# Half of w_out loaded as float32 by SyncE, and q and k of the first tile loaded four tokens a partition

## The chip, the cores and the metric

The kernel runs on one core of one Trainium2 chip. The metric is the device time of one execution in microseconds; the time before is the median of three executions. A span is the time from the first to the last instruction of the one execution that was profiled.

## The reference

Chunked attention (64 tokens attend to the same 64 tokens, in each of 8 heads) is followed by a multiplicative feed-forward stage without a non-linearity, all in float32.

```python
q, k, v: (8, 8, 576, 64)            # batch, heads, tokens, head dim
scores = (1 / sqrt(64)) * q_c @ k_c.T          # per chunk of 64 tokens
attn = exp(scores - max); attn /= (sum(attn) + 1e-9)
x = (attn @ v_c) as (4608, 512)                # tokens, heads * head dim
a = x @ w1 ; b = x @ w2                        # (512, 1024) each
h = (a * b) @ w3                               # (1024, 1024)
out = h @ w_out                                # (1024, 512), float32
```

## The kernel before

The kernel works in bfloat16 with float32 accumulation. The 4608 tokens are 36 groups of 128 tokens, and four groups make one tile of 512 tokens, so there are nine tiles (`TILES`).

Since nothing stands between w3 and w_out, their product is made once on the chip, and the two last matrix products become one. `add_w3o` does this for each of the eight blocks of 128 rows of w3: TensorE transposes the block (L428), a copy brings it to SBUF (`w3t`, L226 or L228, the lines of the copy helper on ScalarE and VectorE), TensorE multiplies it with all of w_out (L439, eight matmuls of 512 columns, cut into two halves by `wo_cut`, each of which waits for its own part of w_out), and a copy stores it as `w3o_sb`.

A group (`add_group`) passes through these steps. q and k for 128 tokens are in `raw`, tokens on the partitions, heads and head dim along the row. For groups 0 to 11 TensorE transposes them (L317, eight transposes of 128x128 into one PSUM buffer `ffn`); later groups are transposed by a DMA that SP issues. k is copied to `kT`. q is copied to `qd`, a block-diagonal arrangement that has been zeroed before, in two copies of 64 partitions. Eight matmuls of 64 columns make the scores (L345), and VectorE and ScalarE do the softmax (L353 to L371). Then the probabilities are transposed (L376, or by a DMA), multiplied with v (L387), and copied to `xt`.

A tile (`add_tile`) multiplies `xt` with w1 and w2 (L471, 64 matmuls of 512 columns), multiplies the two results on VectorE (L480), and multiplies that with `w3o_sb` (L502). Outputs are copied to SBUF, the first twelve over weights that are no longer needed (`kept`), the others to 20 buffers `o_sb`. They are stored by SP after all loads are in (`OUT_AFTER`, `OUT_KEY`).

All loads are issued by POOL (GpSimd), whose DMAs convert float32 to bfloat16 on the way. Their order at the front is the list `LOADS`, written out by hand: the first half of w_out, then q and k of groups 1 and 0, the identity matrix that POOL itself makes, then blocks of w3, the second half of w_out, and so on. `load_qk` loads 128 tokens of q or k: 128 partitions by 8 heads, runs of 64 values.

The order on each engine is not found at run time. `Plan.run` walks through time with a cost for each operation (`cost`, `lag`, `issue`), a queue of eight transfers each for POOL and SP that share the transfer rate, and a key for each operation; at each moment a free engine takes the ready operation with the lowest key. The instructions are then emitted in that order, and each engine carries out its own in order. POOL takes the loads strictly in the order of the list. While the first tokens are not through, the gaps that the plan sees on TensorE are filled with matmuls on zeros (`fills`, L563), fourteen of them at the very start.

Of the kernel before, what the change touches and what calls it, by code (L numbers as in the profile page):

```python
# [16 lines left out]

LOADS = [('wo', 0, 4), ('qk', 1), ('qk', 0), ('ident',), ('w3', 7, 8), ('wo', 4, 8), ('w3', 6, 7), ('qk', 2),
# [3 lines left out]
TILES = [4] * 9  # L22
XT = 16
OUT_AFTER, OUT_KEY = 35, 80
QK_BY_DMA, A_BY_DMA = set(range(12, 36)), set(range(16, 36))
# [19 lines left out]
class Plan:  # L45
# [22 lines left out]
    def run(self):  # L68
        free = {e: 0.0 for e in ("PE", "ACT", "DVE", "POOL", "SP")}
        free["POOL"] = free["SP"] = 1.2  # L70
        todo = {e: [] for e in free}
# [9 lines left out]

        rings, flown = {"POOL": [], "SP": []}, 3.4
        left, now, order, ends = len(self.ops), 0.0, [], [1.2]
        loads = [o for o in self.ops if "POOL" in o.engines]
# [23 lines left out]
        while left or any(rings.values()):  # L108
# [13 lines left out]
            for eng in free:  # L122
                if free[eng] > now or len(rings.get(eng, ())) >= self.RING:
                    continue
                pick = [o for o in (loads[:1] if eng == "POOL" else todo[eng]) if ready(o)]
                if not pick:
                    continue
                o = min(pick, key=lambda o: (o.key, o.place))
                for e in o.engines:
                    todo[e].remove(o)  # L130
                if eng == "POOL":
                    loads.pop(0)
                o.start, o.engine = now, eng
                cost = o.cost[o.engines.index(eng)] if isinstance(o.cost, tuple) else o.cost
                if o.issue:
                    free[eng] = now + o.issue
                    rings[eng].append([free[eng], cost, o])
# [7 lines left out]
                heapq.heappush(ends, free[eng])  # L145
                left -= 1
            while ends and ends[0] <= now:
# [9 lines left out]
def kernel(  # L157
# [20 lines left out]
    B, H, S, D = q.shape  # L178
    C = 64
    NCH = S // C  # L180
    N_TOK = B * S
# [34 lines left out]

    qds = [wpool.tile([P, 2, NM, 2 * C], bf, tag=f"qd{i}", name=f"qd{i}") for i in range(BUFS["qd"])]
    vds = [wpool.tile([P, NM, NCH, 2 * D], bf, tag=f"vd{i}", name=f"vd{i}") for i in range(BUFS["vd"])]
    es = [wpool.tile([P, 8, C + 1], bf, tag=f"e{i}", name=f"e{i}") for i in range(BUFS["e"])]
    halves = [slice(0, C), slice(C, P)]  # L220
# [34 lines left out]
    def load_qk(g):  # L255
# [3 lines left out]
        for w, src in enumerate((q, k)):  # L259
            for r, b, c, n in parts:  # L260
# [4 lines left out]
                box["ops"].append(load(0.45 * n, 0.5 + 0.2 * n, emit, takes=() if box["ops"] else ("raw",)))  # L265

    def load_v(b, y0, y1):
        for t in range(2):
            def emit(eng, t=t):
                nc.gpsimd.dma_start(vds[b % len(vds)][halves[t], 2 * y0:2 * y1, :, t * D:(t + 1) * D].rearrange("p m c d -> p (m c) d"),  # L270
                                    v[b, NM * t + 2 * y0:NM * t + 2 * y1].rearrange("h (c p) d -> p (h c) d", p=C))
            o = load(1.025 * (y1 - y0), 0.5 + 0.335 * (y1 - y0), emit, takes=() if b in v_first else ("vd",),
                     after=(zero_v[b % len(vds)],))
            v_first.setdefault(b, o)
            for y in range(y0, y1):
                v_got.setdefault((b, y), []).append(o)

    def load_w12(j0, j1):
        for dst, w in ((w1_sb, moe_w1), (w2_sb, moe_w2)):
            for t in range(2):  # L280
                def emit(eng, dst=dst, w=w, t=t):
                    nc.gpsimd.dma_start(
                        dst[halves[t], :, j0 * P:j1 * P],
                        w[t * NM * D:(t + 1) * NM * D, j0 * P:j1 * P].rearrange("(m d) n -> d m n", d=D))
                o = load(0.41 * (j1 - j0), 0.62, emit)
        for j in range(j0, j1):
            w12_got[j] = o

    def load_w3(k0, k1):
        def emit(eng):  # L290
            nc.gpsimd.dma_start(w3_sb[:, k0:k1, :], moe_w3.rearrange("(ko p) n -> p ko n", p=P)[:, k0:k1, :])
        o = load(1.45 * (k1 - k0), 0.75, emit)
        for i in range(k0, k1):
            w3_got[i] = o

    def load_wo(k0, k1):
        def emit(eng):
            nc.gpsimd.dma_start(wo_sb[:, k0:k1, :], moe_w_out.rearrange("(ko p) n -> p ko n", p=P)[:, k0:k1, :])
        wo_got.append(load(0.72 * (k1 - k0), 0.75, emit))
        wo_cut.append((k0, k1))  # L300


    x_done = {}

    def add_group(g, kt, ks, ka, kv):
        box = {}
        bc = chunks(g)
        qd = qds[g % len(qds)]

        turned = g in QK_BY_DMA  # L310

        def t_emit(eng):
# [26 lines left out]
        def s_emit(eng):  # L339
            sc = box["sc"] = ps("p_sc", [P, 2, 2, 2, C])  # L340
            for cc in range(2):
# [5 lines left out]

        def flat(x):
            return x.rearrange("p cc y t k -> p (cc y t) k")

        def max_emit(eng):
            nm = box["nm"] = sb("nm", [P, 8, 1], f32, bufs=3)
            nc.vector.tensor_reduce(nm[:, :, 0], flat(box["sc"]), axis=AX.X, op=ALU.max)  # L353

        def sub_emit(eng):
            sd = box["sd"] = sb("sd", [P, 8, C], f32)
            nc.vector.tensor_sub(sd[:], flat(box["sc"]), box["nm"].to_broadcast([P, 8, C]))  # L357

# [33 lines left out]

        got = raws[g]["ops"]
        if turned:
            tr = kc = plan.add("SP", 1.75, kt, qk_turn, after=got, takes=("kqT",), uses=[(got[0], "raw")], lag=3.5, issue=1.3)
            held, cost = [(tr, "kqT")], (0.35, 0.6)
        else:
            tr = plan.add("PE", 0.46, kt, t_emit, after=got + [made_ident], takes=("ffn",), uses=[(got[0], "raw")], lag=0.2)
            held, cost = [(tr, "ffn")], (0.43, 0.66)
            kc = plan.add(("DVE", "ACT"), cost, kt, k_copy, after=(tr,), takes=("kT",), uses=held)  # L400
        q0 = plan.add(("DVE", "ACT"), cost, kt, q_copy(0), after=[tr] + zero_q, takes=("qd",), uses=held)
        q1 = plan.add(("DVE", "ACT"), cost, kt, q_copy(1), after=(tr, q0), uses=held)
        s = plan.add("PE", 0.24, ks, s_emit, after=(kc, q0, q1), takes=("p_sc",), uses=[(kc, "kqT" if turned else "kT"), (q0, "qd")],
                     lag=0.2)
        mx = plan.add("DVE", 0.69, ks, max_emit, after=(s,), lag=0.05)
# [9 lines left out]
        av = plan.add("PE", 0.24, kv, av_emit, after=[ac] + [o for b, _ in bc for y_ in (0, 1) for o in v_got[b, y_]], takes=("p_av",),  # L415
                      uses=[(ac, "at")] + [(v_first[b], "vd") for b in sorted({b for b, _ in bc})], lag=0.2)
        x_done[g] = plan.add(("ACT", "DVE"), 0.68, kv, x_copy, after=(av,), takes=("xt",), uses=[(av, "p_av")])

# [3 lines left out]
    def add_w3o(ko, key):  # L422
# [26 lines left out]
        for i, (k0, k1) in enumerate(wo_cut):  # L449
            mms.append(plan.add("PE", 0.216 * (k1 - k0), key - 0.1 * i, mm_emit(i), after=[tcp, wo_got[i]] + mms,  # L450
                                takes=() if i else ("ffn",), uses=[(tcp, "w3t")], lag=0.2))
# [4 lines left out]
    kept = [w3_sb[:, i:i + 1, :].rearrange("p a n -> p (a n)").bitcast(f32) for i in range(FO)]  # L456
    kept += [wo_sb[:, i:i + 2, :].rearrange("p a n -> p (a n)").bitcast(f32) for i in range(0, FO, 2)]

    def add_tile(g0, n, kab, ko_):
# [33 lines left out]
        for tk, x0, x1 in cols:  # L493
# [30 lines left out]

    made_ident, landing = None, 1.6
    for what, *args in LOADS:
        if what == "ident":
            made_ident = plan.add("POOL", 0.6, 0, lambda eng: make_identity(nc, ident[:]), lag=0.3)
        else:
            {"qk": load_qk, "v": load_v, "w12": load_w12, "w3": load_w3, "wo": load_wo}[what](*args)  # L530
    landing = 2.5
    for g in range(NG):
        if g not in raws:
            load_qk(g)
# [61 lines left out]
```

## Time and profile before

| what | value |
|---|---|
| median of 3 executions | 254.22 us (253.74 to 254.31) |
| the profiled execution | 252.69 us |
| its span | 250.9 us |
| PE (TensorE matmul) busy | 242.0 us, 96% |
| DVE (VectorE) busy | 178.1 us, 71% |
| ACT (ScalarE) busy | 140.2 us, 56% |
| POOL (GpSimd) busy | 102.1 us, 41% |
| read from and written to HBM | 38.80 MB and 9.44 MB |

Busy PE counts the matmuls on zeros too, and a matmul that is waiting in the pipeline, so 96% is not 96% useful work. PEld is the loading of the stationary operand, which overlaps the matmuls. The groups of instructions that the change touches, from the page: line, engine and operation, output and input, shapes and count, then busy us and mean ns of one, then idle time of the engine just before them.

```profile
L264 POOL DMA_DIRECT2D raw<-in_q_dram x40 | 34.3, 858 | 31.4 <-DMA kqT<-raw 11.8
L264 POOL DMA_DIRECT2D raw<-in_k_dram x40 | 34.3, 859 | 20.8 <-DMA vd<-in_v_dram 10.8
L439 PE MATMUL ffn<-wo_sb,w3t 128*128 128x512 bf16 x64 | 15.6, 379 | 0.4 <-DVE w3t L228 0.3
L228 DVE COPY qd<-ffn 64x512 bf16<-64x512 bf16 x14 | 5.9, 419 | 10.4 <-ACT kT L226 10.2
...
wo_sb<-in_moe_w_out_dram POOLq DMA_DIRECT2D x2, 512.0 KB, 7.1
```

The last line is of the DMA issues: the count, the KB of each as written, and the median us from issue to landing. A span is followed by what lies around it, 252.69 - 250.9 = 1.8 us in this execution.

### The profile page before, as it was taken

The page shows a single profiled execution, that of the slowest core. Times are in us where ns is not written, and L with a number is a line of the kernel's source. Part 1 is how long each engine was busy: PE and PEld are TensorE (multiplying, and loading weights), DVE is VectorE, ACT ScalarE, POOL GpSimd, SP SyncE. Part 2 cuts the span into 40 slices and gives each one's busy share as a digit, 9 for nine tenths or more (in the row PEclk, how much of TensorE's full clock was granted, in tenths as well). Part 3 has the DMA queues.
Part 4 walks back from the last instruction along what each step waited for, and adds up shares of the span by engine and source line. Part 5 has one row for each costly group of instructions (what it writes and reads, how often), then busy time and mean ns, then how long its engine had stood idle before and what let it go on. Part 6 is the DMA issues. An engine that isn't in the chain of part 4 may idle for free.

```text
span 250.9 us, 4705 instructions
## 1 busy us (share of the span) xinstructions
PE 242.0 (96%) x1771; PEld 124.8 (50%) x1771; DVE 178.1 (71%) x324; ACT 140.2 (56%) x237; POOL 102.1 (41%) x128
## 2 busy tenths in 40 slices
PE   8699989999999999999999999999999999999994
PEld 2356555555655555554544544554454444444443
DVE  6088866888998898788989888888898762232320
ACT  8057465557877786775546556555565344323222
POOL 8847398987529674347414631720000000000000
PEclk9899999999999999999999999999999999999999
DMA  5999999999999999999999999999998992121114
GB/s 79 170 194 190 158 177 180 172 135 144 125 130 154 145 157 133 157 159 126 157 133 155 156 139 157 141 148 151 125 199 280 357 384 80 42 84 42 43 44 167
DMA packets 160406, 38.06 MB, mean 152 GB/s; under 512 B 149376, under 2 KB 154880, under 8 KB 160384
## 3 DMA queue, kind: packets, MB, share of 16 engines
q0 software_dynamic: 118688, 19.41, 119.5%
q1 hardware_dynamic: 41696, 18.36, 40.0%
q8 instruction: 14, 0.23, 0.4%
q14 instruction: 8, 0.07, 0.1%
HBM read 38.80 MB, written 9.44 MB: 192 GB/s over the span
## 4 chain that ended last, share of the span: by engine, by line
PE 87%; DMA 6%; DVE 3%; ACT 2%; issue 1%; POOL 1%; ACTq 0%; POOLq 0%
PE ffn L471 46%; PE ffn L502 23%; PE ffn L439 5%; DMA at<-an 4%; PE p_sc L345 3%; PE p_av L387 3%; DMA raw<-in_k_dram 2%; PE ffn L317 2%; PE p_av L563 1%; PE ffn L376 1%; PE ffn L428 1%; DVE qd L228 1%; ACT kT L226 1%; DVE xt L228 0%; ACT qd L226 0%
## 5 line engine op out<-in xcount | busy, mean ns | idle before, releaser
L471 PE MATMUL ffn<-xt,w_sb 128*128 128x512 bf16 x576 | 134.5, 379 | 0.0
L471 PEld LDWEIGHTS <-w_sb 128*128 128x128 bf16 x576 | 53.6, 98 | 57.6
L480 DVE TENSOR_TENSOR abT<-a_sb,ffn 128x512 bf16<-128x512 f32 x72 | 48.7, 678 | 30.2 <-PE ffn L471 29.6
L502 PE MATMUL ffn<-w3o_sb,abT 128*128 128x512 bf16 (+2 forms) x304 | 67.6, 368 | 0.0
L226 ACT COPY a_sb<-ffn 128x512 f32<-128x512 f32 x72 | 42.0, 584 | 35.7 <-PE ffn L471 35.3
L264 POOL DMA_DIRECT2D raw<-in_q_dram x40 | 34.3, 858 | 31.4 <-DMA kqT<-raw 11.8
L502 PEld LDWEIGHTS <-abT 128*128 128x128 bf16 x304 | 28.4, 98 | 30.5
L264 POOL DMA_DIRECT2D raw<-in_k_dram x40 | 34.3, 859 | 20.8 <-DMA vd<-in_v_dram 10.8
L365 DVE TENSOR_REDUCE ss<-e 128x8 f32<-128x520 bf16 x36 | 24.8, 689 | 5.1 <-ACT e L361 4.8
L361 ACT ACTIVATE e<-sd 128x512 bf16<-128x512 f32 x36 | 22.8, 634 | 7.2 <-DVE sd L357 6.9
L353 DVE TENSOR_REDUCE nm<-p_sc 128x8 f32<-128x512 f32 x36 | 24.3, 675 | 2.4 <-PE p_sc L345 2.3
L226 ACT COPY qd<-kqT 64x512 bf16<-64x512 bf16 x34 | 20.9, 615 | 7.0 <-DMA kqT<-raw 6.7
L357 DVE TENSOR_TENSOR sd<-p_sc,nm 128x512 f32<-128x512 f32 x36 | 24.6, 684 | 0.3
L371 DVE TENSOR_TENSOR an<-e,rs 128x512 bf16<-128x512 bf16 x36 | 24.6, 684 | 0.2
L226 ACT COPY o_sb<-ffn 128x512 f32<-128x512 f32 (+2 forms) x16 | 8.5, 532 | 24.1 <-PE ffn L502 24.0
L270 POOL DMA_DIRECT2D vd<-in_v_dram x16 | 18.5, 1166 | 4.9 <-DMA raw<-in_q_dram 1.7
L226 ACT CAST xt<-p_av 128x512 bf16<-128x512 f32 x24 | 14.0, 585 | 9.3 <-PE p_av L387 9.2
L387 PEld LDWEIGHTS <-vd 128*128 128x128 bf16 x288 | 12.9, 98 | 8.5 <-issue 1.4
L439 PE MATMUL ffn<-wo_sb,w3t 128*128 128x512 bf16 x64 | 15.6, 379 | 0.4 <-DVE w3t L228 0.3
L387 PE MATMUL p_av<-at,vd 128*128 128x64 bf16 x288 | 14.3, 193 | 0.8 <-DVE xt L228 0.7
L345 PEld LDWEIGHTS <-qd 128*128 128x128 bf16 x288 | 12.2, 98 | 5.6 <-ACT qd L226 1.0
L228 DVE COPY qd<-ffn 64x512 bf16<-64x512 bf16 x14 | 5.9, 419 | 10.4 <-ACT kT L226 10.2
(44 smaller groups left out, 160.9 us busy)
## 6 DMA issues: line engine op xcount, KB each, us to landing
out_dram<-o_sb SPq DMA_DIRECT2D x23, 256.0 KB, 2.7
vd<-in_v_dram POOLq DMA_DIRECT2D x16, 288.0 KB, 12.1
raw<-in_q_dram POOLq DMA_DIRECT2D x32, 128.0 KB, 10.0
raw<-in_k_dram POOLq DMA_DIRECT2D x32, 128.0 KB, 9.5
w_sb<-in_moe_w_dram POOLq DMA_DIRECT2D x8, 256.0 KB, 8.8
w_sb<-in_moe_w_dram POOLq DMA_DIRECT2D x16, 128.0 KB, 4.9
out_dram<-w_sb SPq DMA_DIRECT2D x8, 256.0 KB, 3.0
wo_sb<-in_moe_w_out_dram POOLq DMA_DIRECT2D x2, 512.0 KB, 7.1
```

Of the source, the lines that this page charges most:

```text
L226: nc.scalar.copy(o, i)
L264: nc.gpsimd.dma_start(box["t"][r, w], src[b, :, c * C:(c + n) * C, :].rearrange("h p d -> p h d"))
L353: nc.vector.tensor_reduce(nm[:, :, 0], flat(box["sc"]), axis=AX.X, op=ALU.max)
L357: nc.vector.tensor_sub(sd[:], flat(box["sc"]), box["nm"].to_broadcast([P, 8, C]))
L361: nc.scalar.activation(e[:, :, :C], box["sd"][:], ACT.Exp, scale=scale)
L365: nc.vector.reduce_sum(ss[:], box["e"][:], axis=AX.X)
L371: nc.vector.tensor_mul(an[:], box["e"][:, :, :C], box["rs"].to_broadcast([P, 8, C]))
L387: nc.tensor.matmul(t[:, m, cc, :], vds[b % len(vds)][:, m, c, :], box["at"][:, 2 * cc + y, u * C:(u + 1) * C], start=True, stop=True)
L439: nc.tensor.matmul(box["wp"][:], box["t"][:, ki, :], wo_sb[:, ki, :], start=(ki == wo_cut[0][0]), stop=(ki == wo_cut[-1][1] - 1))
L471: nc.tensor.matmul(t[:, :w], wt[:, ki, j * P:(j + 1) * P], x[:, ki, :], start=(ki == 0), stop=(ki == KO - 1))
L480: nc.vector.tensor_mul(box["abT"][:, j, :w], box["as", j][:, :w], box["b", j][:, :w])
L502: nc.tensor.matmul(t[:, :x1 - x0], box["abT"][:, ki, tk * P:(tk + 1) * P], w3o_sb[:, ki, x0:x1], start=(ki == 0), stop=(ki == FO - 1))
```

## The change

Three things are changed, with the hand-written order that goes with them.

First, w_out's first half (`STAGED = 4` blocks of 128 rows) is no longer loaded by POOL. SP loads each block as float32 into a buffer `o_sb` at the very start, and ScalarE or VectorE casts it to `wo_sb`. Each matmul of the first half at L439 waits for all four casts.

Second, q and k of the first tile (`NQ = 1`) are loaded by `load_quad`. One quad holds four heads and eight chunks, 512 tokens: a partition has four consecutive tokens (`R = 4`) of two heads, runs of 256 values instead of 64. It takes four loads for k and q. Such a quad serves two groups, and a group of the first tile is now four heads of four chunks, instead of eight heads of two chunks. TensorE transposes a quad by 64 columns at a time: k of both groups at once, then q, each 16 transposes of 128x64 that write the upper or the lower 64 partitions. The queries come out in the order (token mod 4, token div 4), so the outputs of the first tile are stored with two DMAs for each 128 rows, rows four apart; the keys are brought back to their natural order where the score matmul reads them.

Third, `LOADS` is a new list that begins with the identity and the first quad, and the plan's numbers are set anew (SP is free from 0.8, a transfer begins `reach` after its issue, the load costs of w1, w2, w3, w_out and v are 2 to 12% lower). There are 16 buffers `o_sb` instead of 20; four outputs more are kept over the quads' buffers.

```diff
-LOADS = [('wo', 0, 4), ('qk', 1), ('qk', 0), ('ident',), ('w3', 7, 8), ('wo', 4, 8), ('w3', 6, 7), ('qk', 2),
-         ('w3', 3, 4), ('w3', 2, 3), ('qk', 3), ('w3', 5, 6), ('w3', 1, 2), ('w3', 0, 1), ('v', 0, 0, 2), ('qk', 4),
-         ('w3', 4, 5), ('w12', 0, 2), ('qk', 5), ('w12', 6, 8), ('w12', 2, 4), ('qk', 6), ('w12', 4, 6), ('qk', 7),
-         ('qk', 8), ('v', 1, 0, 2), ('qk', 9), ('qk', 10)]
+LOADS = [('ident',), ('quad', 0, 0), ('w3', 5, 6), ('w3', 7, 8), ('wo', 4, 8), ('quad', 0, 1), ('w3', 1, 2),
+         ('w3', 6, 7), ('w3', 2, 3), ('w3', 4, 5), ('v', 0, 0, 2), ('qk', 4), ('w3', 3, 4), ('w3', 0, 1), ('qk', 5),
+         ('w12', 0, 2), ('qk', 6), ('w12', 4, 6), ('qk', 7), ('w12', 2, 4), ('w12', 6, 8), ('qk', 8), ('v', 1, 0, 2),
+         ('qk', 9), ('qk', 10)]
+NQ = 1
+STAGED = 4
...
-        free["POOL"] = free["SP"] = 1.2
+        free["POOL"], free["SP"] = 1.2, 0.8
...
-        rings, flown = {"POOL": [], "SP": []}, 3.4
+        rings, flown, reach = {"POOL": [], "SP": []}, 2.2, {"POOL": 1.6, "SP": 1.3}
...
-    BUFS = {"raw": 6, "kqT": 4, "kT": 3, "qd": 3, "vd": 3, "sd": 2, "e": 2, "an": 4, "at": 6, "w3t": 2, "abT": 2,
-            "a_sb": 3, "o_sb": 20, "xt": XT, "ffn": 6, "p_sc": 1, "p_av": 1}
+    BUFS = {"raw": 6, "rawq": 2, "kqT": 4, "kT": 3, "qd": 3, "vd": 3, "sd": 2, "e": 2, "an": 4, "at": 6, "w3t": 2, "abT": 2,
+            "a_sb": 3, "o_sb": 16, "xt": XT, "ffn": 6, "p_sc": 1, "p_av": 1}
...
+    def load_quad(n, y):
+        box = quads[n, y] = {"ops": []}
+        c0 = 8 * n
+        cut = min(8, (c0 // NCH + 1) * NCH - c0)
+        parts = [(c0, 0, cut)] + ([(c0, cut, 8)] if cut < 8 else [])
+        for w, src in ((1, k), (0, q)):
+            for t in range(2):
+                for c, i0, i1 in parts:
+                    def emit(eng, w=w, src=src, t=t, i0=i0, i1=i1):
...
+                        nc.gpsimd.dma_start(box["t"][i0 * C // R:i1 * C // R, w, t],
+                                            src[b, h:h + 2, c * C:(c + i1 - i0) * C, :].rearrange("h (p r) d -> p h (r d)", r=R))
...
+    def stage_wo(k0, k1):
+        staged = []
+        for ki in range(k0, k1):
+            box = {}
+
+            def emit(eng, ki=ki, box=box):
+                box["t"] = sb("o_sb", [P, D_MODEL], f32)
+                nc.sync.dma_start(box["t"][:], moe_w_out[ki * P:(ki + 1) * P])
+
+            def cast(eng, ki=ki, box=box):
+                copy(eng, wo_sb[:, ki, :], box["t"][:])
+
+            o = plan.add("SP", 0.67, -2000 + ki, emit, takes=("o_sb",), lag=1.6, issue=0.1)
+            staged.append(plan.add(("ACT", "DVE"), 0.6, -1500 + ki, cast, after=(o,), uses=[(o, "o_sb")]))
+        wo_got.append(staged)
+        wo_cut.append((k0, k1))
...
+        def quad_turn(w):
+            def emit(eng):
+                tr = raw["tr", w] = ps("ffn", [P, 2, 8 * C], bf)
+                for t in range(2):
+                    for i in range(R):
+                        for u in range(2):
+                            nc.tensor.transpose(tr[halves[u], t, i * P:(i + 1) * P], raw["t"][:, w, t, u, i * D:(i + 1) * D], ident[:])
+            return emit
+
+        def quad_k(eng):
+            box["kT"] = sb("kT", [P, NM, P]).rearrange("p (s a) c -> p s (a c)", s=2).rearrange("p s (r k) -> p s r k", r=R)
+            copy(eng, box["kT"], raw["tr", 1].rearrange("p s (r k) -> p s r k", r=R)[:, :, :, C * hf:C * (hf + 1)])
+
+        def quad_q(u):
+            def emit(eng):
+                copy(eng, qd[halves[u], :, u * C:(u + 1) * C].rearrange("p (cc t) (r k) -> p t cc r k", t=2, r=R),
+                     raw["tr", 0][halves[u]].rearrange("p t (r h cc k) -> p h t cc r k", r=R, h=2, cc=4)[:, hf])
+            return emit
+
+        def quad_s(eng):
+            sc = box["sc"] = ps("p_sc", [P, 8, C])
+            for cc in range(4):
+                for t in range(2):
+                    nc.tensor.matmul(sc[:, 2 * cc + t, :], qd[:, 2 * cc + t, :], box["kT"][:, t, :, cc * C // R:(cc + 1) * C // R].rearrange("p r k -> p k r"),
+                                     start=True, stop=True)
...
+    kept += [t[:, i].rearrange("p a b c -> p (a b c)").bitcast(f32) for t in rawqs for i in range(2)]
...
-                nc.sync.dma_start(out[r0:r0 + P, x0:x1], box["os", tk, x0][:, :x1 - x0])
+                if g0 + tk >= 4 * NQ:
+                    nc.sync.dma_start(out[r0:r0 + P, x0:x1], box["os", tk, x0][:, :x1 - x0])
+                else:
+                    for i in range(2):
+                        nc.sync.dma_start(out[r0 + i * C:r0 + (i + 1) * C].rearrange("(k r) n -> r k n", r=R),
+                                          box["os", tk, x0][halves[i], :])
```

More of the change, by code (lines that the diff above doesn't have):

```diff
@@ L80, in run @@
                     todo[e].append(o)
-        rings, flown = {"POOL": [], "SP": []}, 3.4
-        left, now, order, ends = len(self.ops), 0.0, [], [1.2]
+        rings, flown, reach = {"POOL": [], "SP": []}, 2.2, {"POOL": 1.6, "SP": 1.3}
+        left, now, order, ends = len(self.ops), 0.0, [], [0.8, 1.2]
         loads = [o for o in self.ops if "POOL" in o.engines]
@@ L136, in run @@
                     free[eng] = now + o.issue
-                    rings[eng].append([free[eng], cost, o])
+                    rings[eng].append([free[eng] + reach[eng], cost, o])
                 else:
@@ L145, in run @@
                 heapq.heappush(ends, free[eng])
+                if o.issue:
+                    heapq.heappush(ends, rings[eng][-1][0])
                 left -= 1
@@ L179 @@
     C = 64
+    R = 4
     NCH = S // C
@@ L218 @@
     vds = [wpool.tile([P, NM, NCH, 2 * D], bf, tag=f"vd{i}", name=f"vd{i}") for i in range(BUFS["vd"])]
+    rawqs = [wpool.tile([P, 2, 2, 2, R * D], bf, tag=f"rawq{i}", name=f"rawq{i}") for i in range(BUFS["rawq"])]
     es = [wpool.tile([P, 8, C + 1], bf, tag=f"e{i}", name=f"e{i}") for i in range(BUFS["e"])]
@@ L391, in x_copy @@
             copy(eng, xt[:, :, g % XT * P:(g % XT + 1) * P], box["av"].rearrange("p m cc t -> p m (cc t)"))
-        got = raws[g]["ops"]
-        if turned:
+        emits = (k_copy, q_copy, s_emit, av_emit, x_copy)
+        cost = (0.43, 0.66)
+        if quad:
+            emits = (quad_k, quad_q, quad_s, quad_av, quad_x)
+            got = raw["ops"]
+            if not hf:
+                raw["turns"] = [plan.add("PE", 0.75, kt, quad_turn(w), after=got[:len(got) // (1 + w)] + [made_ident],
+                                         takes=("ffn",), uses=[(got[0], "rawq")], lag=0.2) for w in (1, 0)]
+            trk, tr = raw["turns"]
+            held = [(tr, "ffn")]
+            kc = plan.add(("DVE", "ACT"), cost, kt, emits[0], after=(trk,), takes=("kT",), uses=[(trk, "ffn")])
+        elif turned:
+            got = raws[g]["ops"]
             tr = kc = plan.add("SP", 1.75, kt, qk_turn, after=got, takes=("kqT",), uses=[(got[0], "raw")], lag=3.5, issue=1.3)
@@ L397, in add_group @@
         else:
+            got = raws[g]["ops"]
             tr = plan.add("PE", 0.46, kt, t_emit, after=got + [made_ident], takes=("ffn",), uses=[(got[0], "raw")], lag=0.2)
[L399 to L404, printed above, removed]
+            held = [(tr, "ffn")]
+            kc = plan.add(("DVE", "ACT"), cost, kt, emits[0], after=(tr,), takes=("kT",), uses=held)
+        q0 = plan.add(("DVE", "ACT"), cost, kt, emits[1](0), after=[tr] + zero_q, takes=("qd",), uses=held)
+        q1 = plan.add(("DVE", "ACT"), cost, kt, emits[1](1), after=(tr, q0), uses=held)
+        s = plan.add("PE", 0.24, ks, emits[2], after=(kc, q0, q1), takes=("p_sc",),
+                     uses=[(kc, "kqT" if turned else "kT"), (q0, "qd")], lag=0.2)
         mx = plan.add("DVE", 0.69, ks, max_emit, after=(s,), lag=0.05)
@@ L414, in add_group @@
             ac = plan.add(("DVE", "ACT"), (0.43, 0.66), ka, at_copy, after=(at,), takes=("at",), uses=[(at, "ffn")])
-        av = plan.add("PE", 0.24, kv, av_emit, after=[ac] + [o for b, _ in bc for y_ in (0, 1) for o in v_got[b, y_]], takes=("p_av",),
+        av = plan.add("PE", 0.24, kv, emits[3], after=[ac] + [o for b, _ in bc for y_ in ((y,) if quad else (0, 1)) for o in v_got[b, y_]], takes=("p_av",),
                       uses=[(ac, "at")] + [(v_first[b], "vd") for b in sorted({b for b, _ in bc})], lag=0.2)
-        x_done[g] = plan.add(("ACT", "DVE"), 0.68, kv, x_copy, after=(av,), takes=("xt",), uses=[(av, "p_av")])
+        x_done[g] = plan.add(("ACT", "DVE"), 0.68, kv, emits[4], after=(av,), takes=("xt",), uses=[(av, "p_av")])
     w3o_done = []
@@ L525 @@
     made_ident, landing = None, 1.6
+    if STAGED:
+        stage_wo(0, STAGED)
     for what, *args in LOADS:
@@ L529 @@
         else:
-            {"qk": load_qk, "v": load_v, "w12": load_w12, "w3": load_w3, "wo": load_wo}[what](*args)
+            {"qk": load_qk, "quad": load_quad, "v": load_v, "w12": load_w12, "w3": load_w3, "wo": load_wo}[what](*args)
     landing = 2.5
     for g in range(NG):
-        if g not in raws:
+        if g >= 4 * NQ and g not in raws:
             load_qk(g)
```

42 lines of the change are left out of this document (31 added, 11 removed).

## The prediction

> **What bounds the kernel now.** I read the page's shares and its chain of waits first, then the chain in order of time, then tables of windows, then the timeline of the first 40 us. The lines with a bare start and duration are pieces of the chain; the lines with a window A:B give its length, then PE, PEld, DVE, ACT and POOL busy us (instructions), the granted clock, the DMA share and GB/s.
>
> ```profile
> span 250.9 us, 4705 instructions
> ...
> PE 87%; DMA 6%; DVE 3%; ACT 2%; issue 1%; POOL 1%; ACTq 0%; POOLq 0%
> ...
> 3.02 6.11 DMA raw<-in_k_dram
> 9.17 0.62 PE ffn L317 x8
> 9.79 1.17 PE p_av L563 x4
> 10.96 0.89 PE ffn L317 x8
> 11.85 1.28 PE p_av L563 x3
> 13.13 0.76 PE ffn L428 x8
> 13.91 0.70 DVE w3t L228
> 14.66 1.04 PE ffn L439 x4
> ...
> 34.39 0.42 DVE qd L228
> 34.81 0.60 DVE xt L228
> 35.41 0.60 DVE w3o_sb L228
> 36.01 0.61 DVE xt L228
> ```
>
> TensorE is the bound, and the chain gives its pace: 0.86 us for 4 matmuls of 512 columns (0.216 each), 0.45 for 8 transposes (0.056 each), 0.23 for 8 matmuls of 64 columns (0.029 each). Priced so, the useful work is L471 576 x 0.216 = 124.4, L502 62.2 (280 of 512 columns, and the last tile's narrow ones), L439 64 x 0.216 = 13.8, L345 and L387 576 x 0.029 = 16.7, and 224 transposes 12.5: 229.6 us. The span is 250.9, so 21.3 us are lost, and the question is where.
>
> The chain shows it: nothing useful runs before 9.17, and the pieces at L563 are warm-up matmuls on zeros. Counting the timeline up to 25.0 us: 72 transposes (4.0), 24 score matmuls (0.7) and 26 at L439 (5.6), together 10.3 us of work; 14.7 us are lost by then. About 1.3 more go around 33 to 37 us, where the chain passes over four DVE copies, 1.5 between 55 and 70, 1 in the long middle, and the last 2.8 are the tail. This change can only win in the first 25 us.
>
> ```profile
> 1.26 0.89 POOL L298 DMA_DIRECT2D wo_sb<-in_moe_w_out_dram  x1 [0.81 <-POOLq L580]
> 3.02 0.90 POOL L264 DMA_DIRECT2D raw<-in_k_dram  x1
> ...
> 6.60:9.90 3.30, 1.27 (x12) 0.62 (x11) 0.00 (x0) 0.00 (x0) 3.30 (x6) 1.00 2.39 157
> 38.00:42.00 4.00, 4.00 (x29) 2.21 (x28) 2.67 (x5) 2.81 (x5) 3.71 (x6) 1.00 1.43 189
> ...
> 10.20:13.60 3.40, 3.40 (x21) 0.50 1.14 191
> ...
> 15.00:25.00 10.00, 9.81 (x95) 5.95 (x93) 8.54 (x18) 7.06 (x10) 6.56 (x9) 1.00 1.58 189
> 25.00:33.00 8.00, 7.96 (x75) 4.79 (x74) 6.83 (x13) 4.21 (x7) 4.22 (x8) 1.00 2.35 165
> ```
>
> There the bound is the stream of loads: POOL issues half of w_out (0.52 MB as bfloat16) ahead of the first q and k, and q and k move at 157 GB/s while w1 and w2 move at 189. The clock was granted at half from 10.2 to 13.6, after a stretch with 1.0 us of busy PE in 3.
>
> **The change, part by part.**
>
> *First half of w_out by SP.* POOL loses one issue (0.89). SP gets four loads of 0.26 MB in float32. Other engines start at 0.74 to 0.87 us, so I let SP start at 0.9, against 1.26 on POOL; an SP transfer of that size lands 2.7 us after its issue where the queue is free (the output stores). Reading costs the same bytes of HBM; at 297 to 390 GB/s (the stores from 188 us on) the 1.05 MB take 2.7 to 3.5 us. What is won is the start: I take 0.65 us.
>
> *Casts.* Four of 128x512, to bfloat16: the nearest rows are ACT's w3o cast, 585 ns, and DVE's, 673. Two on each engine is 1.2 to 1.3 us. ACT zeroes vd until 6.15 and then waits 5.7 us for the first transposes; DVE is idle from 5.3 to 12.5. So this costs nothing while the loads land before about 7 us; behind a late load the cast holds its whole engine, and the k and q copies queue behind it: up to 0.9 us, not counted.
>
> *Identity first.* 0.58 us on POOL (5.62 to 6.20) now stands ahead of the first q and k, which POOL starts to issue at 1.84 instead of 2.14.
>
> *Quads.* Eight transfers of 128 KB replace eight of 128 KB, with runs four times as long. Each should move at w12's 189 GB/s, 0.69 us, instead of 0.83: 0.14 x 8 = 1.1 us of the stream, half of it before the first quad is complete. Bounds: no gain, and w3's 210 GB/s, 1.6. Issuing one falls from 0.90 to about the 0.61 of w12's row. One quad serves two groups, so group 1's q and k come with group 0's.
>
> *Arrivals.* Before, w_out's half and four qk transfers were complete when the second set of transposes ran at 10.82. Subtracting 0.65 and 0.56 gives 9.6 for the first quad's q, 8.1 for its k; with SP's loads at the stores' best rate it is a microsecond earlier (8.6 and 7.1, just as the 14 opening fills end at 7.14). Then come w3 block 5 at 9.9 to 11.0, block 7 at 11.3 to 12.3, and w_out's second half at 14.0 to 15.0 (before: 15.4, with one block of w3 fewer ahead of it).
>
> *More transposes.* A quad takes 2 x 2 x 4 x 2 = 32 instead of 16 for the same two groups; tile 0 takes 64 instead of 32. They stream the same 128 columns of the identity, so I price them at 0.056: +1.8 us of PE. No row shows a product with a 64-column stationary operand. From below: two neighbours overlap, one pair in the time of one, +0. From above: the half-clock row, 0.107 (eight in 0.86), +3.3 over the 0.056. I take 0.056, the row with the same shape of moving operand.
>
> [...]
>
> *Copies.* The q copies write and read in runs of 16; DVE's row is 419 ns. At DVE's slower 673, eight would cost 2 us of DVE, spread over 20. At nothing, covered by the slack of two engines.
>
> *Outputs.* Four more SP issues of 0.45 after 185 us, where only stores wait: nothing.
>
> *The sum.* By the time w_out's second half lands PE can have done 32 narrow transposes (1.8), 16 of w3 (0.9), two groups' scores (0.5) and two half sums at L439 (1.7): 4.8, against 1.9 by 15 us before. From there to 25 us are 10 to 11 us, in which PE worked usefully 82% of the time between 15 and 25 before, and 95% after 25. So the work at 25 us is 4.8 + 8.2 = 13.0 to 4.8 + 10.4 = 15.2; without the 1.8 that are new, 11.2 to 13.4, against 10.3. Gain 0.9 to 3.1; I take 2.0, and 0.3 back between 33 and 70 us, where the loads of later groups come no earlier than the stream. Net 1.7: span 250.9 - 1.7 = 249.2. The profiled run took 252.69 in all, the median of the shown runs is 254.22, 3.3 over the span; so 252.5.
>
> **Rivals.**
>
> *Narrow transposes overlap.* Then 1.8 comes off: 250.7. For: two neighbours write different halves of the partitions. [...] Against: no row shows it here.
>
> *Narrow transposes are slow (slower than before).* At 0.107 each, 64 x 0.051 = 3.3 more, of which the wait of about 1.5 us for q hides 0.8: 252.5 + 2.5 = 255.0. It decides from a spacing of 0.056 + 1.7 / 64 = 0.083. [...]
>
> *DVE and ACT become the bound.* They were busy 15.6 of 20 us from 15 to 25, and the chain at 34 to 37 already runs over DVE copies. If they set the pace, the earlier data wait for softmax and copies, and the front gain goes, the extra transposes being hidden: 254.2. Against: the two also start about 3 us earlier.
>
> *The clock halves again at 10.2.* The 3.1 us of PE work due there would run into 15.0 instead of 14.0: 253.5. For: the row at 0.50. Against: PE is busier ahead of it. [...]
>
> **How the numbers follow.** Forecast 0.50, overlap 0.10, slow transposes 0.17, DVE and ACT 0.15, clock 0.08. Predicted time 252.5, the forecast's own range 251.2 to 253.9. The range for all, 250.2 to 255.3, reaches past the overlap and the slow transposes. A measurement of this kernel can tell about 0.2%, 0.5 us, from no change. Faster takes most of the forecast (0.46), overlap, most of clock and a third of DVE/ACT: 0.64; same 0.12, mostly from DVE/ACT; slower 0.24.
>
> **What would show it.** First quad transposes at 7.1 to 8.1 and 8.6 to 9.6; starts 0.056 apart inside a set (0.028 or 0.107: a rival); quad loads at 0.69 each; casts done before 8 us; the first L428 at 9.9 to 11 instead of 12.9; useful PE work at 25 us of 13.0 to 15.2. The forecast is wrong if that is under 12.1, or if the front wins 2 us and the stretch from 33 to 70 us loses them.

## The result and the profile after

The change made the kernel slower by 1.3%: 257.67 us median (256.79 to 259.16, 4 executions) against 253.98 (252.99 to 254.31, 4 executions), a ratio of 1.0133 with a 95% interval of 1.0086 to 1.0181. The median lies outside the predicted range of 250.2 to 255.3, and on the other side of no change. The profiled span is 255.0 us. Ratios, here and below, leave out executions that took over 1.5% longer than the fastest one of the same kernel.

The page's span and the shares of its chain:

```profile
span 255.0 us, 4731 instructions
...
PE 88%; DMA 6%; DVE 2%; POOL 1%; issue 1%; ACT 1%; POOLq 0%
```

The shares are nearly those of before; they do not show the loss. From the table of groups by shape, the first 45 us, two that are new (busy us, mean ns of one, then idle time before them):

```profile
L383 PE MATMUL p_sc<-kT,qd 128*128 128x64 bf16 x32 | 4.2, 287 | 0.7 <-ACT qd L232 0.7
L366 PEld LDWEIGHTS <-rawq 128*64 128x64 bf16 x64 | 2.0, 109 | 2.7 <-DMA rawq<-in_k_dram 1.5 <-DMA rawq<-in_q_dram 0.7 <-issue 0.4
```

Score matmuls of 287 ns, where those of before have 193, stand out. The timeline of the front, in order of time, with start and duration first:

```profile
6.06 2.23 ACT L232 CAST wo_sb<-o_sb 128x512 bf16<-128x512 f32 x4
...
7.46 0.25 PEld L366 LDWEIGHTS <-rawq 128*64 128x64 bf16 x8 [1.02 <-DMA rawq<-in_k_dram]
...
10.87 0.62 PE L523 MATMUL ffn<-ident,w_sb 128*128 128x128 bf16 x8 [0.56 <-DMA w_sb<-in_moe_w_dram]
...
19.17 0.48 PEld L366 LDWEIGHTS <-rawq 128*64 128x64 bf16 x16 [0.42 <-issue]
```

The data come when they were expected: the first quad's k at 7.5, the first block of w3 at 10.9 instead of 12.9. The last line has the loads for 16 narrow transposes in 0.48 us, 0.030 each.

The loss is far from the front. In the chain of waits there is one long piece between 184 and 198 us:

```profile
186.28 10.38 DMA at<-an
196.66 0.05 issue
196.71 0.41 PE p_av L470 x8
```

The timeline of SP shows what was ahead of it (a line with SPq is an issue on SP; x8 is eight of them):

```profile
180.38 5.80 SPq L612 DMA_DIRECT2D out_dram<-w_sb  x8
186.28 2.62 SPq L412 DMA_TRANSPOSE at<-an  x1
```

A transpose of probabilities, issued at 186.28, lands 10.4 us later. TensorE has done all else it was given by about 193, and waits for 3.6 us. The eight DMAs issued just before are the first tile's outputs. First four windows of the changed kernel, then one of the kernel before while it stores (length, PE, PEld, DVE, ACT, POOL, clock, DMA share, GB/s; the DMA share is the mean busy share of the core's 16 DMA engines):

```profile
182.00:186.00 4.00, 3.95 (x27) 1.90 (x25) 3.79 (x8) 1.75 (x4) 0.00 (x0) 1.00 0.25 64
190.00:193.00 3.00, 3.00 (x15) 1.21 (x13) 1.98 (x4) 1.99 (x4) 0.00 (x0) 1.00 1.16 104
190.00:196.60 6.60, 3.12 (x15) 1.21 (x13) 3.30 (x6) 1.99 (x4) 0.00 (x0) 1.00 0.94 192
196.70:200.00 3.30, 3.29 (x24) 1.55 (x25) 1.38 (x2) 0.58 (x1) 0.00 (x0) 0.64 1.07 390
```

```profile
185.80:189.30 3.50, 3.50 (x38) 1.89 (x35) 3.18 (x7) 1.97 (x5) 0.00 (x0) 1.00 1.07 328
```

From 182 to 186 us almost nothing but these outputs moves: the DMA share is 0.25, the packet time of 4.0 of 16 engines, at 64 GB/s. From 190 to 193 it is 104 GB/s (a share above 1, as the 1.16 there, means that packets' times overlap, and then it counts no engines). In the kernel before it is 328 GB/s. From 190.0 to 196.6 PE is busy for 3.12 of 6.60 us.

The wait seems to have a second cost. In the clock records the granted clock is at half from 197.6 to 201.0 us, just behind the wait (the last window of the four shows 0.64), and on the chain eight matmuls at L598 take 3.02 us from 197.35, where eight take 1.73 at the full clock. The 3.4 us at half cost an estimated 1.7 us of PE's work. With the 3.6 us of waiting that makes 5.3, and the changed kernel is 5.4 us behind x1 below, which has neither. The traces of x4 and x11, the only others with the wait, have a lower clock there as well: 0.76 in x4's window from 200 to 205 us, 0.73, 0.50 and 0.50 in x11's from 196 to 201, 201 to 206 and 206 to 211. It is 1.00 in the windows of x1, x2 and x3 from 180 to 205 us, of x5 and x6 from 180 to 197, and of x7, x8, x10 and the kernel before from 25 to 205.

### The profile page after: what moved, and what is told of

It is laid out like the page before. It is cut to its first block, busy times and chain, and to the rows that moved or that the text cites. A ratio compares the mean times of both kernels' runs of the same rounds, so it can differ in the third digit from the quotient of the medians.

```text
span 255.0 us, 4731 instructions
## 1 busy us (share of the span) xinstructions
PE 242.4 (95%) x1764; PEld 126.6 (50%) x1795; DVE 176.3 (69%) x317; ACT 145.3 (57%) x248; POOL 100.2 (39%) x127
## 4 chain that ended last, share of the span: by engine, by line
PE 88%; DMA 6%; DVE 2%; POOL 1%; issue 1%; ACT 1%; POOLq 0%
PE ffn L567 47%; PE ffn L598 24%; PE ffn L534 5%; DMA at<-an 4%; PE p_sc L431 3%; PE p_av L470 3%; DMA rawq<-in_q_dram 2%; PE p_sc L383 1%; PE ffn L402 1%; PE ffn L459 1%; PE ffn L523 1%; POOL rawq L289 1%; DVE qd L234 1%; ACT qd L232 0%; PE p_av L390 0%
## 5 line engine op out<-in xcount | busy, mean ns | idle before, releaser
L567 PE MATMUL ffn<-xt,w_sb 128*128 128x512 bf16 x555 | 132.1, 380 | 1.1
L598 PE MATMUL ffn<-w3o_sb,abT 128*128 128x512 bf16 (+2 forms) x298 | 67.9, 373 | 0.4
L598 PEld LDWEIGHTS <-abT 128*128 128x128 bf16 x304 | 28.3, 99 | 30.2 <-issue 1.1
L270 POOL DMA_DIRECT2D raw<-in_q_dram x36 | 30.7, 856 | 28.2 <-DMA vd<-in_v_dram 15.4
L270 POOL DMA_DIRECT2D raw<-in_k_dram x36 | 30.7, 854 | 23.5 <-DMA vd<-in_v_dram 11.3
L232 ACT COPY o_sb<-ffn 128x512 f32<-128x512 f32 (+2 forms) x19 | 10.3, 540 | 30.1 <-PE ffn L598 30.1
L232 ACT COPY qd<-kqT 64x512 bf16<-64x512 bf16 x37 | 22.7, 614 | 0.3
L470 PEld LDWEIGHTS <-vd 128*128 128x128 bf16 x256 | 11.6, 98 | 10.7 <-DMA at<-an 4.1
L534 PE MATMUL ffn<-wo_sb,w3t 128*128 128x512 bf16 x62 | 16.1, 399 | 0.1
L470 PE MATMUL p_av<-at,vd 128*128 128x64 bf16 x256 | 12.7, 193 | 3.6 <-DMA at<-an 3.6
L431 PEld LDWEIGHTS <-qd 128*128 128x128 bf16 x256 | 10.9, 98 | 5.0 <-DVE qd L234 0.7
L234 DVE CAST xt<-p_av 128x512 bf16<-128x512 f32 x12 | 8.3, 688 | 5.0 <-PE p_av L470 4.9
```

Source lines behind the costliest of these rows:

```text
L232: nc.scalar.copy(o, i)
L270: nc.gpsimd.dma_start(box["t"][r, w], src[b, :, c * C:(c + n) * C, :].rearrange("h p d -> p h d"))
L470: nc.tensor.matmul(t[:, m, cc, :], vds[b % len(vds)][:, m, c, :], box["at"][:, 2 * cc + y, u * C:(u + 1) * C], start=True, stop=True)
L534: nc.tensor.matmul(box["wp"][:], box["t"][:, ki, :], wo_sb[:, ki, :], start=(ki == wo_cut[0][0]), stop=(ki == wo_cut[-1][1] - 1))
L567: nc.tensor.matmul(t[:, :w], wt[:, ki, j * P:(j + 1) * P], x[:, ki, :], start=(ki == 0), stop=(ki == KO - 1))
L598: nc.tensor.matmul(t[:, :x1 - x0], box["abT"][:, ki, tk * P:(tk + 1) * P], w3o_sb[:, ki, x0:x1], start=(ki == 0), stop=(ki == FO - 1))
```

## The experiments

Theory S: the row pattern of the new stores is at fault. `rearrange("(k r) n -> r k n")` has a leading count of 4, and the window from 182 to 186 us has the packet time of 4.0 of 16 engines; the theory takes the one to set the other, and the transposes on the same queue to wait behind these four. Its rivals: Q, the eight issues instead of four; H, scattered rows are slow in HBM; P, the new plan itself. Edits are shown against the changed kernel, for x4 against the kernel before; "..." stands for lines left out.

**x1_half_stores.** The same eight issues, plain halves.

```diff
-                        nc.sync.dma_start(out[r0 + i * C:r0 + (i + 1) * C].rearrange("(k r) n -> r k n", r=R),
+                        nc.sync.dma_start(out[r0 + i * C:r0 + (i + 1) * C],
```

> The changed kernel with the first tile's outputs stored as two halves of 64 contiguous rows each, instead of rows four apart; the same eight issues on SP. Its first 512 output rows stand in another order than the reference's. Theory S (the row pattern whose leading count is 4 puts each store on a quarter of the DMA engines, at some 100 GB/s instead of 390, and the attention transposes queue behind them): the stores of 180 to 186 us move at over 300 GB/s, the 10.4 us landing of a transposed probability tile and the 3.6 us wait of PE for it go, span 249.5 to 251.0. Theory Q (it is the count of issues: eight on SP instead of four delay the transposes by about 3 us): the wait stays, span 254 to 255.5.

Measured: 252.25 us, ratio to before 0.9914 (0.9859 to 0.9969). The wait is gone, and Q falls. The rate was a miss: an issue of 0.13 MB takes 0.63 us, which is some 200 GB/s, and from 186 to 190 us 190 GB/s move. The profiled span, 251.2, is just above what was expected.

**x2_nat_x.** The copy to `xt` puts the tokens in order, so that the stores are plain.

```diff
-            copy(eng, xt[:, 2 * y:2 * y + 2, x0:x0 + 4 * C], box["av"].rearrange("p u cc t -> p u (cc t)"))
+            copy(eng, xt[:, 2 * y:2 * y + 2, x0:x0 + 4 * C].rearrange("p u (ck r) -> p u ck r", r=R).rearrange("p u (cc k) r -> p u cc r k", cc=4),
+                 box["av"].rearrange("p u cc (r k) -> p u cc r k", r=R))
...
```

> The changed kernel, but the copy to xt puts the first tile's tokens back in their natural order, so that each 128 rows are stored by one plain DMA. Both theory S and theory Q expect the stall at 186 to 197 us to go: span 249.5 to 251.0. A third, P (the new plan set the transposes too late, whatever the stores do), expects it to stay: 254 to 255.5. If the strided copy costs, the mean of the first tile's copies to xt rises over 585 ns on ACT and 680 on DVE.

Measured: 252.12 us, ratio 0.9903 (0.9848 to 0.9958). P falls too. The strided copies cost: 1.28 us on DVE, 1.30 on ACT, where the changed kernel has 0.68 and 0.59.

**x3_nat_xk.** x2, and in addition k in natural order in `kT`, written with gaps by the copy.

```diff
-            copy(eng, box["kT"], raw["tr", 1].rearrange("p s (r k) -> p s r k", r=R)[:, :, :, C * hf:C * (hf + 1)])
+            copy(eng, box["kT"].rearrange("p s (k r) -> p s r k", r=R), raw["tr", 1].rearrange("p s (r k) -> p s r k", r=R)[:, :, :, C * hf:C * (hf + 1)])
...
-                    nc.tensor.matmul(sc[:, 2 * cc + t, :], qd[:, 2 * cc + t, :], box["kT"][:, t, :, cc * C // R:(cc + 1) * C // R].rearrange("p r k -> p k r"),
+                    nc.tensor.matmul(sc[:, 2 * cc + t, :], qd[:, 2 * cc + t, :], box["kT"][:, t, cc * C:(cc + 1) * C],
...
```

> As the run before, and k is put in its natural order by the copy after the transposes, so that the score matmul reads its moving operand without gaps. If the gaps (64 elements apart) are what makes the first four groups' eight score matmuls take 0.9 to 1.05 us instead of 0.23 to 0.40, they return to 0.23 to 0.40; four times 0.65, 2.6 us of PE, is saved, and as PE has little slack there, 1.5 to 2.6 us of the span against the run before: 247 to 249. If PE waits for other things in the front anyway, under 0.5.

Measured: 252.11 us, ratio 0.9898 (0.9842 to 0.9955), no gain on x2. In the table of groups the score matmuls are cheap again, and the copies dear:

```profile
L383 PE MATMUL p_sc<-kT,qd 128*128 128x64 bf16 x32 | 1.6, 194 | 1.3 <-ACT qd L232 1.1 <-DVE sd L441 0.2
L234 DVE COPY kT<-ffn 128x512 bf16<-128x512 bf16 x1 | 1.3, 1297 | 6.1 <-ACT kT L232 6.1
L232 ACT CAST xt<-p_av 128x512 bf16<-128x512 f32 x1 | 1.3, 1296 | 0.0
```

The copy of k stands on the chain (three pieces at `ACT kT`, 1.20 to 1.32 us, in the first 23 us), so it seems that what the matmuls saved was paid there; x7 bears this out.

**x4_before_scatter.** The kernel before, with only the stores changed.

```diff
-                nc.sync.dma_start(out[r0:r0 + P, x0:x1], box["os", tk, x0][:, :x1 - x0])
+                if g0:
+                    nc.sync.dma_start(out[r0:r0 + P, x0:x1], box["os", tk, x0][:, :x1 - x0])
+                else:
+                    for i in range(2):
+                        nc.sync.dma_start(out[r0 + i * C:r0 + (i + 1) * C].rearrange("(k r) n -> r k n", r=4),
+                                          box["os", tk, x0][halves[i], :])
```

> The kernel before, with nothing changed but the first tile's stores: two DMAs for each 128 rows, rows four apart, as in the changed kernel (its first 512 output rows stand in another order). The plan and the order are those of before. Theory S: the stores slow to some 100 GB/s, a transposed probability tile lands late, and 3 to 6 us are lost between 186 and 205 us: span 254 to 257. If the stall is the new plan's alone: 250.5 to 251.5.

Measured: 258.22 to 262.3 us in four executions, ratio 1.0178 (1.0087 to 1.0269), 4.5 us on 254.2; the profiled span is 258.1, beyond what was expected. Its chain has the same long piece as the changed kernel:

```profile
193.52 9.28 DMA at<-an
```

So the stores alone, in an otherwise unchanged kernel, bring the loss.

**x5_lead16.** Scattered rows again, 16 apart, with a leading count of 16.

```diff
-                        nc.sync.dma_start(out[r0 + i * C:r0 + (i + 1) * C].rearrange("(k r) n -> r k n", r=R),
+                        nc.sync.dma_start(out[r0 + i * C:r0 + (i + 1) * C].rearrange("(r k) n -> k r n", r=R),
```

> The changed kernel, but each half store walks its 64 output rows as 16 by 4, the rows of a step 16 apart, instead of 4 by 16 with rows 4 apart; as many issues, as many bytes, rows as scattered (the first 512 output rows stand in another order). Theory S (a leading count of 4 means 4 of the 16 DMA engines): the stores of 180 to 186 us move at over 300 GB/s, no wait of PE, 251.5 to 253. Theory H (scattered rows are slow in HBM): still near 100 GB/s and 256 to 259.

Measured: 251.51 us, ratio 0.9916 (0.9880 to 0.9952). No wait of PE; the rate is 166 GB/s from 186 to 190 us, where the issues, 0.75 us each, would give an estimated 175, so that part of the expectation was a miss. H falls: rows as scattered as before do no harm.

**x6_read_x.** x2 with the copy's walk turned round, so that the gaps are on the side of PSUM.

```diff
-            copy(eng, xt[:, 2 * y:2 * y + 2, x0:x0 + 4 * C], box["av"].rearrange("p u cc t -> p u (cc t)"))
+            copy(eng, xt[:, 2 * y:2 * y + 2, x0:x0 + 4 * C].rearrange("p u (ck r) -> p u ck r", r=R).rearrange("p u (cc k) r -> p u cc k r", cc=4),
+                 box["av"].rearrange("p u cc (r k) -> p u cc k r", r=R))
...
```

> As x2_nat_x, but the copy to xt walks its output without gaps and reads PSUM with gaps, instead of the other way round. In x2 these four copies took 1.28 to 1.30 us instead of 0.59 to 0.68. If it is the writing of 2 bytes every 8 that costs, they return to 0.6 to 0.75 and the run is 0 to 1.5 us faster than x2 (250.6 to 252.1 against 254.2 of before). If any walk with gaps costs, they stay at 1.3.

Measured: 250.56 us, ratio 0.9885 (0.9839 to 0.9931); the copies are back at 0.68 us on DVE and 0.59 on ACT. The time is at the lower end of what was expected, and the intervals can't tell it from that of x2.

**x7_read_xk.** x3 with both copies that way.

```diff
...
-            copy(eng, box["kT"], raw["tr", 1].rearrange("p s (r k) -> p s r k", r=R)[:, :, :, C * hf:C * (hf + 1)])
+            copy(eng, box["kT"].rearrange("p s (k r) -> p s k r", r=R), raw["tr", 1].rearrange("p s (r k) -> p s k r", r=R)[:, :, C * hf:C * (hf + 1), :])
...
```

> As x3_nat_xk, both copies walking their output without gaps and reading PSUM with gaps. If writing with gaps was what made the k copies 1.3 us (0.42 to 0.59 before), they return to 0.45 to 0.7; PE then keeps the 2.6 us that x3 gave back in the copies, 249.5 to 251.5. If reading with gaps costs as much: as x3, 252.1.

Measured: 248.76 us (248.44 to 249.55, 6 runs), ratio 0.9805 (0.9770 to 0.9840). This beats both kernels, and is below the 249.5 to 251.5 that was expected. The groups by shape:

```profile
L232 ACT COPY kT<-ffn 128x512 bf16<-128x512 bf16 x6 | 3.5, 589 | 1.5 <-PE ffn L403 1.1 <-PE ffn L366 0.3
L234 DVE CAST xt<-p_av 128x512 bf16<-128x512 f32 x3 | 2.0, 678 | 0.0
L383 PE MATMUL p_sc<-kT,qd 128*128 128x64 bf16 x32 | 1.6, 194 | 0.9 <-ACT qd L232 0.7 <-DVE sd L441 0.2
L234 DVE COPY kT<-ffn 128x512 bf16<-128x512 bf16 x2 | 1.1, 555 | 3.6 <-ACT kT L232 3.6
```

On ACT a read with gaps costs nothing (589 ns; 586 to 588 without). On DVE the k copy takes 0.69 instead of 0.42 us; the mean of 555 mixes one of each.

**x8_staged_only.** No quads: only w_out by SP, the new list and the new plan numbers.

```diff
-LOADS = [('ident',), ('quad', 0, 0), ('w3', 5, 6), ('w3', 7, 8), ('wo', 4, 8), ('quad', 0, 1), ('w3', 1, 2),
+LOADS = [('ident',), ('qk', 1), ('qk', 0), ('w3', 5, 6), ('w3', 7, 8), ('wo', 4, 8), ('qk', 2), ('qk', 3), ('w3', 1, 2),
...
-NQ = 1
+NQ = 0
```

> The changed kernel without quads: w_out's first half by SP with casts, the identity first, the new list and the new plan numbers, but q and k of the first tile in four loads of 128 tokens each, as before, in the quads' places, and plain stores. If the earlier start of the stream (0.65 us) and the removed issue (0.89 on POOL) are what the front gained: 252.5 to 253.5 against 254.2. If the gain is the quads' (shorter transposes, a better rate, two groups at once): 254 to 255.

Measured: 251.19 us, ratio 0.9899 (0.9843 to 0.9954): lower than either range. The staging with its list and plan numbers is worth about 2.6 us (1.2 to 4.0), as much as was forecast for the whole change or more.

**x9_late_stores.** The scattered stores unchanged, but last.

```diff
...
-        plan.add("SP", 0.7, max(c.key, OUT_KEY + i), emit, after=[c] + raws[OUT_AFTER]["ops"],
+        plan.add("SP", 0.7, max(c.key, OUT_KEY + i), emit, after=[c] + raws[OUT_AFTER]["ops"] + [outs[26][0]] * (i < 4 * NQ),
```

> The changed kernel with all eight scattered stores of the first tile kept as they are, but issued by SP after the last transpose of probabilities. Theory S, with the loss lying in what queues behind them: they still move at about 100 GB/s, 11 us in all, but nothing waits for them: 251 to 252.5, as x1. If slow stores cost by themselves wherever they stand (they hold buffers, or the end waits for them): 254 to 258.

Measured: 251.46 us, ratio 0.9909 (0.9873 to 0.9945), as x1. On SP's queue:

```profile
198.78 1.19 SPq L412 DMA_TRANSPOSE at<-an  x1
...
207.29 5.82 SPq L612 DMA_DIRECT2D out_dram<-w_sb  x8
```

The last transpose is out before the slow stores; nothing waits behind them, and they cost nothing.

**x10_quads_fixed_only.** x7 with w_out's first half on POOL again.

```diff
-LOADS = [('ident',), ('quad', 0, 0), ('w3', 5, 6), ('w3', 7, 8), ('wo', 4, 8), ('quad', 0, 1), ('w3', 1, 2),
+LOADS = [('ident',), ('wo', 0, 4), ('quad', 0, 0), ('w3', 5, 6), ('w3', 7, 8), ('wo', 4, 8), ('quad', 0, 1), ('w3', 1, 2),
...
-STAGED = 4
+STAGED = 0
...
```

> As x7_read_xk (quads, natural order by copies that read with gaps, plain stores), but w_out's first half is loaded by POOL as before, ahead of the first quad; no casts. x7 took 248.8 and x8, staging without quads, 251.2, against 254.1 of before. If the two parts add up, the quads alone are worth 5.3 - 2.9 = 2.4 us: 251.7. If the quads only pay because the first data come early (the two need each other): 252.5 to 254. If they are worth the most: under 251.

Measured: 250.8 us, ratio 0.9867 (0.9835 to 0.9899). This is the third case, under 251. Staging without quads (x8) gives 1.0%, quads without staging 1.3%, and both together (x7) 2.0%. But x8 and x10 share the new order of the other loads and the new plan numbers, which were not tried alone, so what these give is counted in both; and the intervals are too wide to tell the 0.3% by which the sum differs from nothing.

**x11_lead2.** The scattered stores with a leading count of 2.

```diff
-                        nc.sync.dma_start(out[r0 + i * C:r0 + (i + 1) * C].rearrange("(k r) n -> r k n", r=R),
+                        nc.sync.dma_start(out[r0 + i * C:r0 + (i + 1) * C].rearrange("(k r) n -> r k n", r=2),
```

> The changed kernel, each half store walking its 64 rows as 2 by 32 with rows 2 apart (the first 512 output rows stand in another order); same issues and bytes. Theory S, the leading count sets how many of 16 DMA engines work: a count of 4 gave 100 GB/s, 2 gives 50, the 1.05 MB take 21 us instead of 10.5, the transpose behind them lands about 10 us later than in the changed kernel, and the time is 262 to 270 against 257.7. If it is only the gaps between rows, 2 apart is no worse than 4 apart: 252 to 258.

Measured: 267.82 us, ratio 1.0553 (1.0454 to 1.0652). A window while the stores drain:

```profile
186.00:191.00 5.00, 5.00 (x38) 2.51 (x37) 4.77 (x9) 3.43 (x7) 0.00 (x0) 1.00 0.14 48
```

48 GB/s with a leading count of 2, 64 to 104 with 4, and a DMA share of 0.14, 2.2 of 16 engines, against 0.25, 4.0 of 16: the rate and the busy engines go with the count, although the rows stand closer together. SP itself is held by its eight issues from 181.2 to 195.2, and the transpose behind them lands at 206.5, 9.8 us later than in the changed kernel. Theory S expected this; the gaps between rows alone would have left it at 252 to 258.

## Why the prediction was wrong

**The step that failed** is "Outputs": "Four more SP issues of 0.45 after 185 us, where only stores wait: nothing." The issues were counted, the pattern of rows was not, and it was not true that only stores wait there. In the kernel before, SP already issues transposes of probabilities between its stores, and TensorE needs each of them:

```profile
189.33 1.38 SPq L327 DMA_TRANSPOSE at<-an  x1
...
197.52 1.24 SPq L327 DMA_TRANSPOSE at<-an  x1
...
203.99 1.28 SPq L327 DMA_TRANSPOSE at<-an  x1
...
206.00 1.22 SPq L327 DMA_TRANSPOSE at<-an  x1
```

In the changed kernel the eight stores of 1.05 MB drain from 182 to about 194 us, 12 us; at the 328 GB/s of before it would be an estimated 3. The transpose that is queued behind them lands when the last of its packets does. In the trace's packet records 382 of its 512 packets start from 188 to 190 us, and the other 130, a quarter, only from 193.5 to 195, when the scattered rows run out. With the stores' pattern alone undone (x1) the time is 5.4 us less; with the pattern alone added to the kernel before (x4) it is 4.5 us more.

The runs tie the rate to the leading count on the side of the output. With a count of 4 the traces have 4.0 busy engines and 64 GB/s from 182 to 186 us, and 104 GB/s from 190 to 193; a quarter of the 390 GB/s that plain stores reach from 196.7 to 200 us would be an estimated 98. With a count of 2 they have 2.2 busy engines and 48 GB/s, and with 16 a DMA share of 0.51, 166 GB/s and no wait of PE. Other counts were not run, and how a DMA comes by its engines no trace shows.

**The front came near its forecast, and by luck.** The gain without the outputs was put at 1.7 us, a time of 252.5; x1 measures 252.25, which is 0.86% or 2.2 us (0.8 to 3.6) below the kernel before. But by its own sign, under 12.1 us of useful work at 25 us, the forecast of the front is wrong as well: one price was 1.8 us too high, another of 2.7 us was missing, nothing was won by 25 us in the profile, and the gain came later, where a loss was forecast. The prediction also took it that 0.2% can be told from no change; the interval of the result is 0.5% to each side.

- Arrivals: k expected at 7.1 to 8.1, q at 8.6 to 9.6, w3 at 9.9 to 11.0, w_out's second half by 14.0 to 15.0. The trace has sets of transposes at 7.47, 8.23, 8.90 and 9.57, 0.67 to 0.77 apart (0.69 a load was expected), w3 at 10.87, and POOL's wait for w_out ends at 14.86. Right.
- Casts at nothing: all four went to ACT, 6.06 to 8.29 us, with no idle time before them, a little past the 8 us expected. Right in effect, though not two on each engine: the first k copy, at 8.69, waited for TensorE and not for them.
- Narrow transposes at 0.056, +1.8 us: wrong. They run at 0.030, so that 64 of them cost what 32 cost before. This was the first rival: in the trace two neighbours start 3 to 4 ns apart, and the next two mostly 52 to 53 ns later. A load of 64 columns lasts 109 ns, one of 128 columns 98, but the spacing is 0.030.
- Score matmuls: priced as before, 0.23 us for eight, since the text saw eight matmuls of 64 columns and took them as equal. Wrong: eight take 0.9 us on the chain, 0.11 each, four times: 2.7 us of PE more. Their moving operand is read with 128 bytes between neighbours. That this is the cause is shown by x3 and x7, where the same matmuls without gaps are back at 194 ns each instead of 287. Why the gaps slow them no trace shows.
- Useful work at 25 us: 13.0 to 15.2 was expected (from terms a tenth or two off: the first sum is 4.9 and not 4.8, and 10.3 less 1.9 is 84% of 10 us and not 82%), and under 12.1 was to count against the forecast. Counted as before, with 0.030 for a narrow transpose and 0.029 for a score matmul, the changed kernel has done 1.9 + 2.7 + 0.7 + 4.8 (22 matmuls at L534) = 10.1, against 10.3 before. So by 25 us nothing was won in this execution: the gaps in k took 2 us by then, and the clock was at half from 13.3 to 16.7:

```profile
13.30:16.70 3.40, 3.40 (x21) 2.00 (x19) 1.54 (x3) 1.54 (x2) 1.42 (x2) 0.50 1.39 197
```

- The 0.3 us to be given back between 33 and 70 us were on the wrong side. PE's idle time from 25 to 70 us was 0.79 + 0.89 = 1.7 us before (25 to 40 and 55 to 70) and 0.31 + 0.10 + 0.16 = 0.6 after. Counting each load of a stationary operand at the prices above, both kernels have done 41.0 us of useful work at 55 us; at 70 us it is 56.2 in the changed kernel and 55.0 before, at 180 us 166.9 and 165.5. So the profiled gain arises between 55 and 70 us. In the kernel before, the chain stands at copies of ACT and DVE from 53.6 to 55.8 and from 65.8 to 67.0 us, in the changed kernel it does not. This is read from one trace of each; that the earlier loads relieved the copies is a guess.

**The rivals.** Overlapping transposes came true, with a chance of 0.10. Slow transposes, the case on the slower side, did not. DVE and ACT as the bound appear only in places: the changed kernel's chain stands at their work from 10.0 to 12.1, 19.3 to 21.8 and 36.4 to 38.5 us, and in x3 at the slower copies. The clock at half did come, at 13.3 instead of 10.2 us; it also came in the kernel before, and in the profile of x7 it did not, though that kernel opens with the same instructions. What it costs was not tried, and the mean clocks on record don't settle it: one half window of 3.4 us brings the mean to 0.993; x9's two executions at 1.000 took 250.7 and 250.8 us and its four at 0.993 took 251.1 to 252.6, but of the kernel before, measured beside x5, five at 1.000 took 253.3 to 254.1 and seven at 0.993 took 252.5 to 255.8.

## What to carry to other kernels

Read the shape of a rearranged DMA's leading dimension before its number of issues or bytes: x11, the changed kernel and x5 store the same bytes with counts of 2, 4 and 16, take 267.82, 257.67 and 251.51 us, and only the last is harmless. A slow transfer is priced by what is queued behind it: the same eight stores cost 5.4 us ahead of a transpose (257.67 against 252.25 in x1), an estimated 1.7 of it by the half clock behind the wait, and nothing at the end of the queue (x9, 251.46). When data come in another order, let a copy out of PSUM restore it, reading with gaps and writing without (0.59 to 0.69 us a copy in x6 and x7, against 1.28 to 1.30 the other way round in x2 and x3).

## What the hardware showed

- Stores from SP with a leading count of 4 kept 4.0 of 16 DMA engines busy from 182 to 186 us (64 GB/s; 104 from 190 to 193), with a count of 2 2.2 of 16 (48 GB/s). With a count of 16 the same bytes went at 166 GB/s, with 0.75 us to an issue.
- Transposes of 64 columns into the two halves of the partitions, in turn, were 0.030 us apart, transposes of 128 columns 0.056.
- A moving operand with 128 bytes between neighbours took 0.11 us for 64 columns, without gaps 0.029.
- A copy of 128x512 out of PSUM that writes a bfloat16 every 8 bytes took 1.28 to 1.30 us on both engines. Reading with gaps and writing without, ACT took 0.59 as ever, and DVE 0.68 from float32 as ever, and 0.69 instead of 0.42 from bfloat16.
